# One PSUM ring of eight banks, bank-wise exp, larger loads and a new list of steps in a windowed-attention and gated-MLP kernel

## The chip, the cores and the metric

The kernel runs on one core of a Trainium2 chip. The metric is the device time of one execution in microseconds (us), lower is better. The engines are TensorE (PE in the profile, its weight loads PEld), VectorE (DVE), ScalarE (ACT), GpSimd (POOL) and SyncE (SP), which here only issues DMAs. Each engine works through its own instructions in order.

## What is computed

Eight batches of 576 positions go through causal attention with a window of 64 (8 heads of 64), and the result, laid out as 576 x 512, goes through a gated MLP with a spatial mixing matrix.

```python
scores = (1.0 / np.sqrt(D)) * np.matmul(q, k.transpose(0, 1, 3, 2))
mask = (rel >= 0) & (rel < 64)                     # rel = query position - key position
scores = np.where(mask, scores, -1000000000.0)
attn = softmax(scores)
x = np.matmul(attn, v)                             # (8, 8, 576, 64) -> (8, 576, 512)
h = np.maximum(x @ w_in, 0.0)                      # 512 -> 1024
u, vv = h[..., :512], h[..., 512:]
v_n = (vv - mean(vv)) / np.sqrt(var(vv) + 1e-06)   # over the last axis
v_s = np.einsum('ts,bsd->btd', w_spatial, v_n) + b_spatial[None, :, None]
out = (u * v_s) @ w_out                            # 512 -> 512
```

Inputs and output are float32; the kernel computes in float16 with float32 sums.

## The kernel before

The kernel is a set of named steps and one list, `ORDER`, which is written out by hand into the program: each word of it is a step, the engine that takes it, and the buffer numbers that it acquires (`S0_0:PE:0:1`). The steps are emitted in that order, so the list fixes the order of every engine's instructions; semaphores for the dependencies follow from the buffers.

The names of the steps, b the batch, g the group of four heads, u the pair of heads:

- `ldq`, `ldk` (L401), `ldv` (L422): loads of Q, K (one DMA of 576 KB for four heads) and V (five DMAs for four heads, one per 128 positions, in runs of 256 bytes). `ldwin`, `ldwsp`, `ldwo`, `ldb`: loads of the weights and the bias (L327, L343, L384, L352). All loads are issued by SP's queue, marked `DQ`.
- `cq`, `ck`: cast of Q, K to float16 (L293, L296, L301, depending on the engine); `tq`, `tk`: transpose on DVE (L408). `cv`: cast of V; `sl`, `su`, `s4`: copies of V shifted by 64 positions into `hs`.
- `S` (L470): scores of four heads, each head in a PSUM bank of its own. Two banks form a `pair` tile, and there are two pairs. `E` (L477): exp of one pair, 128 x 1024, on ACT. `M` (L480): mask by a minimum on DVE. `Z` (L493): sums over keys by a matmul with ones; `N`, `n` (L519, L521): log and exp of minus the log, that is, the reciprocal. `P` (L504): attention times V; `X` (L512): times the reciprocal. Steps with `_r` are the last 64 queries of a batch (L539, L549, L553, L562, L575, L583).
- `V` (L653, L666): the half of x @ w_in that is normalised, j = 0..3 for 128 positions each and j = 4 for the last 64; `Vr` (L633): relu on ACT; `Vb`, `Va` (L635, L637): mean and variance on DVE; `L1`, `L2` (L680, L682): one over the deviation; `A` (L692): normalisation on DVE. `U` (L708, L713): the other half, transposed; `Ur` (L721): relu. `W`, `We`: transpose of w_spatial on PE and its copies. `G` (L738, L744): spatial mixing; `Ge` (L752): times u. `O` (L763): output product; `Oe` (L610): copy to SBUF; `st`: store. `V_4` of a batch also computes the last 64 rows of the output of the batch before it (L669).
- `D` (L791): warm-up matmuls on a zero tile, which nothing reads.

PSUM holds eight banks: two pairs for the scores and four single banks for everything else. Loads of Q, K and of the weights share eight buffers `nat`; V has four buffers `natv` of four heads.

The list begins with Q and K of batch 0, then mixes V of batch 0 with Q and K of batch 1 and the weights:

```
ldq0_0:DQ:0 ldk0_0:DQ:1 D14:PE:0 ldk0_1:DQ:2 ldq0_1:DQ:3 D12:PE:1 ldv0_00:DQ:0 ldq1_0:DQ:4 D23:PE:2
ldk1_0:DQ:5 ldv0_10:DQ:1 D15:PE:3 cq0_0:POOL:0 ldv0_11:DQ D22:PE:0 D6:PE:1 tq0_0:DVE:0 D0:PE:2
```

Of the kernel before, what the change touches and what calls it, by code (L numbers as in the profile page):

```python
# [29 lines left out]
cv0_11:DVE ldwin001:DQ S1_0:PE:0:1 sl0_11:DVE X0_00:DVE:0 D20:PE:2 cwin110:POOL ldwin010:DQ:4  # L30
E1_00:ACT:1 s40_1:DVE D19:PE:0 ldwin011:DQ su0_11:POOL X0_01:DVE ldwsp3:DQ:5 E1_01:ACT:0 M1_00:DVE
cwin111:POOL P0_10:PE:1 P0_11:PE:2 X0_10:DVE:1 D18:PE:0 cwin100:ACT cwin101:POOL ldwsp2:DQ:7 D3:PE:3
n0_r:ACT X0_11:DVE cwin000:ACT Z1_00:PE:1 M1_01:DVE ldwsp1:DQ:6 P0_r:PE:0 cb:ACT V0_1:PE:3
X0_r:DVE:0 V0_2:PE:2 ck1_1:POOL:2 ldwsp4:DQ:0 Vr0_1:ACT:0 N1_00:ACT:5 Vb0_1:DVE:0 V0_0:PE:0
# [807 lines left out]
```

## Time and profile before

| | |
|---|---|
| median of 3 runs | 203.19 us (202.53 to 204.65) |
| span of the profiled execution | 201.0 us, first to last instruction; its device time is not listed apart, the median of the runs lies 2.2 us above the span |
| busy PE / PEld / DVE / ACT / POOL | 188.6 / 97.7 / 161.2 / 167.0 / 76.5 us |
| HBM read and written | 32.79 MB and 9.44 MB |

A row of the profile names the line, the engine, the operation, and out<-in with the shapes. A timeline row begins with its start and its length in us and merges instructions of one line that follow each other (x3 is three of them); what stands in brackets is the idle time before it and what ended it. Rows of stretches have no names in front; their columns are explained where they are shown.

### The profile page before, as it was taken

The page shows a single profiled execution, that of the slowest core. Times are in us where ns is not written, and L with a number is a line of the kernel's source. Part 1 is how long each engine was busy: PE and PEld are TensorE (multiplying, and loading weights), DVE is VectorE, ACT ScalarE, POOL GpSimd, SP SyncE. Part 2 cuts the span into 40 slices and gives each one's busy share as a digit, 9 for nine tenths or more (in the row PEclk, how much of TensorE's full clock was granted, in tenths as well). Part 3 has the DMA queues.
Part 4 walks back from the last instruction along what each step waited for, and adds up shares of the span by engine and source line. Part 5 has one row for each costly group of instructions (what it writes and reads, how often), then busy time and mean ns, then how long its engine had stood idle before and what let it go on. Part 6 is the DMA issues. An engine that isn't in the chain of part 4 may idle for free.

```text
span 201.0 us, 7008 instructions
## 1 busy us (share of the span) xinstructions
PE 188.6 (94%) x2927; PEld 97.7 (49%) x2927; DVE 161.2 (80%) x307; ACT 167.0 (83%) x307; POOL 76.5 (38%) x144
## 2 busy tenths in 40 slices
PE   7588889899999999989999999999999999999992
PEld 2233535545445445654455545554465455444450
DVE  4699979999998999699699898979957796647430
ACT  2588799878999899897998989999999999457431
POOL 5202575675894398153757999000000000000000
PEclk9999999999999999999999999999999999999998
DMA  6997999899898876999859995897633004200345
GB/s 221 387 276 184 336 378 210 292 372 377 185 274 255 246 221 188 295 243 234 311 118 262 241 316 178 227 284 249 185 111 117 3 5 132 108 0 0 128 145 202
DMA packets 50275, 42.69 MB, mean 212 GB/s; under 512 B 39361, under 2 KB 39489, under 8 KB 50242
## 3 DMA queue, kind: packets, MB, share of 16 engines
q1 hardware_dynamic: 50018, 41.91, 70.1%
q8 instruction: 23, 0.38, 0.8%
q10 hardware_dynamic: 224, 0.33, 0.5%
q14 instruction: 10, 0.08, 0.1%
HBM read 32.79 MB, written 9.44 MB: 210 GB/s over the span
## 4 chain that ended last, share of the span: by engine, by line
PE 70%; DMA 9%; SPq 7%; ACT 5%; DVE 5%; POOL 1%; issue 1%; POOLq 0%
PE bank L738 16%; PE bank L653 12%; PE bank L763 12%; PE bank L708 10%; DMA nk<-in_k_dram 9%; SPq L422 4%; PE pair L470 4%; PE bank L504 3%; PE bank L666 3%; PE bank L493 3%; PE bank L744 2%; SPq L327 2%; ACT e L477 1%; PE bank L713 1%; ACT ob L610 1%
## 5 line engine op out<-in xcount | busy, mean ns | idle before, releaser
L738 PE MATMUL bank<-wspT,vn 128*128 128x512 f16 (+1 forms) x160 | 37.5, 379 | 0.0
L477 ACT ACTIVATE e<-pair 128x1024 f16<-128x1024 f32 x32 | 31.9, 1027 | 2.7 <-PE pair L470 2.5
L752 DVE TENSOR_TENSOR g<-bank,ru 128x512 f16<-128x512 f32 (+1 forms) x40 | 24.8, 632 | 11.0 <-PE bank L738 5.0
L708 PE MATMUL bank<-x,win 128*128 128x512 f16 x128 | 31.6, 379 | 0.0
L763 PE MATMUL bank<-wout,g 128*128 128x512 f16 x128 | 31.3, 379 | 0.0
L653 PE MATMUL bank<-win,x 128*128 128x512 f16 x128 | 30.4, 379 | 0.2 <-DVE x L512 0.2
L721 ACT ACTIVATE ru<-bank 128x512 f32<-128x512 f32 (+1 forms) x40 | 21.4, 562 | 8.4 <-PE bank L708 4.6
L635 DVE BATCH_NORM_STATS2 st<-vs 128x6 f32<-128x512 f16 (+1 forms) x40 | 25.9, 670 | 3.0 <-ACT vs L633 2.8
L512 DVE TENSOR_TENSOR x<-bank,lz 128x512 f16<-128x512 f32 x32 | 21.2, 683 | 5.4 <-PE bank L504 2.6
L633 ACT ACTIVATE vs<-bank 128x512 f16<-128x512 f32 (+1 forms) x40 | 22.9, 597 | 3.1 <-PE bank L653 2.3
L610 ACT COPY ob<-bank 128x512 f32<-128x512 f32 (+1 forms) x39 | 22.6, 588 | 3.3 <-PE bank L763 3.1
L738 PEld LDWEIGHTS <-vn 128*128 128x128 f16 (+1 forms) x160 | 14.9, 97 | 17.7 <-DVE vn L692 0.5
L480 DVE TENSOR_TENSOR e<-e,mask 128x1024 f16<-128x1024 f16 x32 | 22.5, 721 | 1.0 <-ACT e L477 1.0
L408 DVE STREAM_TRANSPOSE qT<-hq 128x576 f32<-128x576 f32 x16 | 19.7, 1243 | 2.5 <-POOL hq L296 2.3
L296 POOL CAST hq<-nq 128x384 f16<-128x384 f32 x33 | 16.5, 536 | 13.1 <-DMA nq<-in_q_dram 12.5
L408 DVE STREAM_TRANSPOSE kT<-hk 128x576 f32<-128x576 f32 x16 | 20.0, 1247 | 1.4 <-ACT hk L293 1.1
L519 ACT ACTIVATE lz<-bank 128x512 f32<-128x512 f32 x32 | 18.6, 603 | 2.1 <-PE bank L493 2.0
L521 ACT ACTIVATE lz<-lz 128x512 f32<-128x512 f32 x32 | 19.6, 631 | 0.1
L653 PEld LDWEIGHTS <-x 128*128 128x128 f16 x128 | 12.0, 97 | 14.3 <-issue 0.6
L708 PEld LDWEIGHTS <-win 128*128 128x128 f16 x128 | 11.9, 98 | 14.4 <-issue 1.3
L763 PEld LDWEIGHTS <-g 128*128 128x128 f16 x128 | 11.8, 98 | 13.4 <-issue 0.5
L692 DVE TENSOR_SCALAR vn<-vs,mv,ln 128x512 f16<-128x512 f16 (+1 forms) x40 | 15.4, 436 | 3.5 <-ACT ln L682 3.3
(85 smaller groups left out, 294.7 us busy)
## 6 DMA issues: line engine op xcount, KB each, us to landing
nq<-in_q_dram SPq DMA_DIRECT2D x16, 576.0 KB, 6.4
nk<-in_k_dram SPq DMA_DIRECT2D x16, 576.0 KB, 5.5
nv<-in_v_dram SPq DMA_DIRECT2D x64, 128.0 KB, 4.9
out_dram<-ob SPq DMA_DIRECT2D x14, 512.0 KB, 4.6
wi<-in_moe_w_in_dram SPq DMA_DIRECT2D x8, 256.0 KB, 5.6
ws<-in_moe_w_spatial_dram SPq DMA_DIRECT2D x4, 288.0 KB, 8.2
nv<-in_v_dram SPq DMA_DIRECT2D x16, 64.0 KB, 3.6
wo<-in_moe_w_out_dram SPq DMA_DIRECT2D x4, 256.0 KB, 7.1
```

The source lines that it names most:

```text
L408: d = add(f"t{name}{b}_{g}", ("DVE", 1.09), key, lambda e: nc.vector.transpose(qt.t[:, :].rearrange("p (i j) -> p j i", j=18), h.t[:, :].b ...
L477: ex = add(f"E{b}_{g}{u}", ("ACT", 0.91), key, lambda e, u=u: nc.scalar.activation(e2[u].t[:, :, :], sc[u].t[:, :, :], AF.Exp, bias=0.0, s ...
L480: mins.append(add(f"M{b}_{g}{u}", ("DVE", 0.65), key, lambda e, u=u: nc.vector.tensor_tensor(e2[u].t[:, :, :], e2[u].t[:, :, :], mask[:, : ...
L610: lambda e: (nc.vector.tensor_copy if last else nc.scalar.copy)(view(), m.t[rows, 0:n]),
L633: rl = add(f"Vr{b}_{j}", ("ACT", 0.49), key, lambda e: nc.scalar.activation(vs.t[0:jn, :], m.t[0:jn, :], AF.Relu), deps=[pv], acq=[vs], us ...
L635: s1 = add(f"Vb{b}_{j}", ("DVE", 0.6), key + 0.02, lambda e: nc.vector.bn_stats(st6.t[0:jn, 0:6], vs.t[0:jn, :]), deps=[rl], acq=[st6], us ...
L653: nc.tensor.matmul(m.t[:, :], xr(b, r)[:, 128 * j:128 * j + 128], w_in_sb[r][:, 512:1024], start=(r == 0), stop=(r == 3))
L708: nc.tensor.matmul(m.t[:, :], w_in_sb[r][:, 128 * i:128 * i + 128], xr(b, r), start=(r == 0), stop=(r == 3))
L721: lambda e, m=m, ru=ru, n=n: nc.scalar.activation(ru.t[:, 0:n], m.t[:, 0:n], AF.Relu), deps=[pu], acq=[ru], uses=[m])))
L738: nc.tensor.matmul(m.t[:, :], w[0:kn, 128 * i:128 * i + 128], wspT[kk][0:kn, 0:512], start=(kk == 0), stop=(kk == 4))
L752: lambda e, m=m, g=g, ru=ru, n=n: nc.vector.tensor_tensor(g.t[:, 0:n], m.t[:, 0:n], ru.t[:, 0:n], ALU.mult),
L763: nc.tensor.matmul(m.t[:, :], G[r][0].t[:, 128 * j:128 * j + 128], w_out_sb[r][:, :], start=(r == 0), stop=(r == 3))
```

## The change

- PSUM becomes eight single banks, and every step takes any of them. A score step takes four banks, and exp works on one bank at a time: `E1_00` to `E1_03`, 128 x 512 each, and four of 128 x 128 for the last queries. The mask still works on two heads at once and waits for both exps.
- A weight load covers two blocks (512 KB, or 576 KB of w_spatial) where it was one. V is loaded for eight heads per DMA (two buffers `natv` of eight heads), for batch 0 in two groups of four heads as before. V's copies are one step per two blocks and eight heads; on POOL each is issued block by block.
- The first V steps of batch 0 are emitted in two halves, `V0a` (rows of w_in that meet heads 0 to 3) and `V0b`.
- 48 warm-up steps of one matmul take the place of 25 of two.
- The list is a new one. Q and K of batch 0 are followed by V of batch 0, the weights `win1`, `wsp`, Q of batch 1, `win0` and the rest of batch 1. In the steady part the order of all steps differs.

The heart of the diff:

```diff
 ORDER = """
-ldq0_0:DQ:0 ldk0_0:DQ:1 D14:PE:0 ldk0_1:DQ:2 ldq0_1:DQ:3 D12:PE:1 ldv0_00:DQ:0 ldq1_0:DQ:4 D23:PE:2
...
+ldk0_0:DQ:0 ldq0_0:DQ:1 ldk0_1:DQ:2 cq0_0:DVE:0 ck0_0:POOL:1 tk0_0:DVE:0 ldq0_1:DQ:3 tq0_0:DVE:1
+ldv0_00:DQ:0 D0:PE:0 D1:PE:1 D2:PE:2 D3:PE:3 D4:PE:4 D5:PE:5 D6:PE:6 D7:PE:7 D8:PE:0 D9:PE:0
...
+D21:PE:0 D22:PE:0 D23:PE:0 D24:PE:0 D25:PE:0 D26:PE:0 S0_0:PE:0:1:2:3 ck0_1:POOL:2 ldv0_01:DQ
+ldv0_10:DQ cq0_1:ACT:3 tk0_1:DVE:2 ldv0_11:DQ E0_00:ACT:0 ldv0_12:DQ cv0_00:ACT:0 E0_02:ACT:1
+ldv0_02:DQ ldv0_13:DQ tq0_1:DVE:3 ldv0_03:DQ cv0_10:DVE E0_03:ACT sl0_00:POOL:0 E0_01:ACT D27:PE:4
+D28:PE:4 D29:PE:4 D30:PE:4 D31:PE:4 D32:PE:4 S0_1:PE:4:5:6:7 M0_00:DVE D33:PE:0 D34:PE:0
+S0_r:PE:0:2:3:1 ldv0_04:DQ E0_12:ACT:2 ldv0_14:DQ E0_10:ACT:3 sl0_10:DVE E0_r0:ACT:0 ldwin10:DQ:4
+M0_01:DVE E0_11:ACT su0_00:POOL E0_13:ACT ldwin11:DQ:5 E0_r1:ACT ldwsp1:DQ:6 cv0_11:DVE D35:PE:6
+Z0_00:PE:6 D36:PE:4 Z0_01:PE:4 M0_10:DVE N0_00:ACT:0 M0_11:DVE cv0_01:DVE s40_0:DVE s40_1:DVE
+su0_11:DVE N0_01:ACT:1 su0_01:DVE E0_r2:ACT ldb:DQ:7 sl0_01:DVE n0_00:ACT D37:PE:0 D38:PE:0
+Z0_10:PE:0 D39:PE:5 Z0_11:PE:5 E0_r3:ACT su0_10:DVE ldwsp0:DQ:0 cwsp3:POOL N0_10:ACT:2 n0_01:ACT
+M0_r:DVE cwin100:ACT D40:PE:7 D41:PE:7 D42:PE:7 P0_00:PE:7 N0_11:ACT:3 sl0_11:DVE P0_01:PE:2
+P0_10:PE:6 Z0_r:PE:4 X0_00:DVE:0 P0_11:PE:3 n0_10:ACT cwin101:DVE N0_r:ACT:4 X0_01:DVE n0_11:ACT
+X0_10:DVE:1 ldwsp2:DQ:1 cwsp2:ACT cwin110:ACT ldq1_0:DQ:2 ldwin01:DQ:3 ldwin00:DQ:4 X0_11:DVE
+cwin111:DVE P0_r:PE:1 cwin001:POOL D43:PE:0 D44:PE:0 D45:PE:0 V0a_3:PE:0 cwsp0:DVE cwsp1:DVE
+ldk1_0:DQ:6 V0a_0:PE:7 n0_r:ACT V0a_1:PE:5 cb:ACT cwsp4:ACT D46:PE:2 V0b_1:PE V0b_0:PE V0b_3:PE
+V0a_2:PE:2 X0_r:DVE:0 Vr0_1:ACT:0 cq1_0:DVE:0 Vr0_3:ACT:1 cwin000:POOL Vr0_0:ACT:2 V0b_2:PE
...
-NWARM = 25
-BUFS = {"nat": 8, "natv": 4, "hqk": 4, "qkT": 6, "hv": 4, "hs": 4, "e2": 4, "er": 2, "lz": 6,
+NWARM = 48
+BUFS = {"nat": 8, "natv": 2, "hqk": 4, "qkT": 6, "hv": 2, "hs": 2, "e2": 4, "er": 2, "lz": 6,
...
-    PAIR = [psp.tile([128, 2, 512], f32, name=f"pair{i}") for i in range(2)]
-    SINGLE = [psp.tile([128, 512], f32, name=f"bank{i}") for i in range(4)]
+    BANKS = [psp.tile([128, 512], f32, name=f"bank{i}") for i in range(8)]
...
-        elif e == "POOL" and len(i.shape) == 4 and i.shape[1] > 2:
-            for lo, hi in ((0, 2), (2, i.shape[1])):
-                nc.gpsimd.tensor_copy(o[:, lo:hi, :, :], i[:, lo:hi, :, :])
+        elif e == "POOL" and len(i.shape) == 4 and i.shape[2] == 8:
+            for c in range(i.shape[1]):
+                nc.gpsimd.tensor_copy(o[:, c, :, :], i[:, c, :, :])
...
+                ld = add(f"ldwin{half}{g}", ("DQ", 0.4), kk,
+                         lambda e, st=st, g=g, cs=cs: nc.sync.dma_start(
+                             st.t[:, 0:1024].rearrange("p (f c) -> p f c", f=2),
+                             moe_w_in[256 * g:256 * g + 256, cs].rearrange("(f p) c -> p f c", f=2)),
+                         acq=[st], nbytes=1.6, n=256)
...
+        groups = [(0, 4), (4, 8)] if b == 0 else [(0, 8)]
...
+                         lambda e, c=c, sn=sn, h0=h0, h1=h1: nc.sync.dma_start(
+                             nv.t[0:sn, c, h0:h1, :],
+                             v[b, h0:h1, 128 * c:128 * c + sn, :].transpose([1, 0, 2])),
...
-            ex = add(f"E{b}_{g}{u}", ("ACT", 0.91), key, lambda e, u=u: nc.scalar.activation(
-                e2[u].t[:, :, :], sc[u].t[:, :, :], AF.Exp, bias=0.0, scale=0.125),
-                deps=[s], acq=[e2[u]], uses=[sc[u]])
+            ex = []
+            for w in (0, 1):
+                ex.append(add(f"E{b}_{g}{2 * u + w}", ("ACT", 0.48), key,
+                              lambda e, u=u, w=w: nc.scalar.activation(
+                                  e2[u].t[:, w, :], sc[2 * u + w].t[:, :], AF.Exp, bias=0.0,
+                                  scale=0.125),
+                              deps=[s] + ex, acq=[] if w else [e2[u]],
+                              uses=[sc[2 * u + w]] + ([e2[u]] if w else [])))
...
+            if b == 0:
+                halves = []
+                for f in (0, 1):
+                    def emit_H(e, j=j, m=m, f=f):
+                        with nc.named_scope(f"V{b}_{j}"):
+                            for r in (2 * f, 2 * f + 1):
+                                nc.tensor.matmul(m.t[:, :], xr(b, r)[:, 128 * j:128 * j + 128],
+                                                 w_in_sb[r][:, 512:1024], start=(r == 0), stop=(r == 3))
...
-            for _ in range(2):
-                nc.tensor.matmul(m.t[:, :], scratch[:, 0:128], scratch[:, :], start=True, stop=True)
-        add(f"D{i}", ("PE", 0.43), -2.0, emit_D, acq=[m], mode="f")
+            nc.tensor.matmul(m.t[:, :], scratch[:, 0:128], scratch[:, :], start=True, stop=True)
+        add(f"D{i}", ("PE", 0.22), -2.0, emit_D, acq=[m], mode="f")
```

Further on in the new list PE's order is: `V0_4`, the five `W`, `U0_4`, `U0_0` to `U0_3`, `S1_0`, `G0_1`, `G0_0`, `S1_1`, `G0_3`, `S1_r`, `Z1_00`, `Z1_01`, `G0_2`, `G0_4`, `Z1_11`, `Z1_r`, `Z1_10`, `O0_0`, `O0_3`, `O0_2`, `P1_r`, `P1_00`, `P1_10`, `P1_01`, `V1_4`, `P1_11`, `O0_1`, `S2_0`, `U1_4`, `V1_0`. DVE has, between the last `A0` and `V1_0`: `tq1_1`, `tk1_1`, the five masks of batch 1, the five `Ge0`, `cv1_0`, `su1_0`, `cv1_1`, `su1_1`, `tk2_0`, `tq2_0` and the five `X1`. Behind U0's casts POOL has `ck1_0`, `ck1_1`, three `cwo`, `ck2_0`, `sl1_1`, `cq2_0`, `cq2_1`, `ck2_1`. All of batch 0's `O` steps stand ahead of `V1_0`; in the old list they stand behind it.

More of the change, by code (lines that the diff above doesn't have):

```diff
@@ L30 @@
[L30 to L34, printed above, removed]
-Vr0_2:ACT:1 tk1_1:DVE:0 cq1_1:POOL:3 ldv1_00:DQ:2 V0_3:PE:3 Vr0_0:ACT:2 n1_00:ACT ldwsp0:DQ:2
@@ L455, in att_steps @@
     def att_steps(b, g, key):
[L456 removed]
+        sc = [buf("bank", f"sc{b}_{g}{hh}") for hh in range(4)]
         e2 = [buf("e2", f"e2_{b}_{g}{u}") for u in (0, 1)]
@@ L527, in rem_steps @@
     def rem_steps(b, key):
-        sc = [buf("pair", f"scr{b}_{u}") for u in (0, 1)]
+        sc = [buf("bank", f"scr{b}_{hh}") for hh in range(4)]
         def emit_S(e):
```

402 lines of the change are left out of this document (206 added, 196 removed).

## The prediction

> **What bounds the kernel now.** I read the page's head and engine shares first, then busy time by stretches, then the order of time on each engine in the first 50 us, then the DMA queue.
>
> ```profile
> span 201.0 us, 7008 instructions
> PE 188.6 (94%) x2927; PEld 97.7 (49%) x2927; DVE 161.2 (80%) x307; ACT 167.0 (83%) x307; POOL 76.5 (38%) x144
> ...
> 0.00:10.00 10.00, 6.68 (x83) 2.90 (x84) 5.80 (x17) 4.11 (x4) 3.74 (x14) 1.00 0.82 303
> 10.00:20.00 10.00, 8.42 (x164) 3.84 (x162) 9.87 (x19) 8.80 (x15) 1.14 (x2) 1.00 0.93 231
> 20.00:30.00 10.00, 8.62 (x136) 4.35 (x137) 8.64 (x14) 8.89 (x16) 6.40 (x12) 1.00 1.02 358
> 30.00:40.00 10.00, 9.16 (x196) 5.54 (x196) 9.94 (x26) 8.71 (x20) 6.01 (x10) 1.00 1.01 250
> ...
> 46.76:196.60 149.84, 148.66 (x2202) 76.97 (x2203) 120.31 (x225) 130.93 (x247) 54.78 (x99) 1.00 0.64 186
> ...
> 130.00:170.00 40.00, 39.91 (x591) 21.05 (x590) 31.27 (x62) 39.44 (x71) 0.00 (x0) 1.00 0.44 136
> ```
>
> The columns are the stretch, its length, the busy time of PE, PEld, DVE, ACT and POOL, then granted clock, DMA share and GB/s. From 46.76 on PE idles 1.2 us of 149.8, at full granted clock. In the last row ACT is 99% busy and PE still idles only 0.1: a nearly full ACT does not hold PE up if the list feeds it well. So the back is PE's own work, and the change does not take matmuls out of it. What can be won lies in the first 47 us, where DVE and the DMA queue are full and PE waits or runs warm-up matmuls.
>
> ```profile
> 8.67 0.76 PE L470 MATMUL pair<-qT,kT 32*64 32x128 f16 x64 [2.05 <-DVE kT L408]
> 24.62 3.63 PE L653 MATMUL bank<-win,x 128*128 128x512 f16 x16
> 39.91 0.76 PE L744 MATMUL bank<-wspT,vn 128*128 128x64 f16 x20 [0.40 <-DVE wspT L301]
> 46.76 2.75 PE L653 MATMUL bank<-win,x 128*128 128x512 f16 x12 [0.18 <-DVE x L512]
> 196.47 0.63 PE L776 MATMUL bank<-wout,g 128*64 128x256 f16 x8
> 147.13 0.47 PE bank L713 x16
> 193.09 3.47 PE bank L763 x16
> ```
>
> These are the milestones: first scores S0_0 at 8.67, V0 at 24.62, G0 at 39.91, V1 at 46.76, last matmul at 196.47. The last two rows (from the chain) price a U step of the 64-row rest at 0.47 and four O steps at 3.47, so 0.87 for one full step of four matmuls. When V1 starts at 46.76, none of the four O0 steps has run.
>
> **The change, part by part.** I lay the new list out by hand up to the first V1 step, with these rows.
>
> ```profile
> 4.84 1.40 POOL L296 CAST hq<-nq 128x384 f16<-128x384 f32 x3 [1.64 <-DMA nq<-in_q_dram]
> 6.13 1.15 ACT L293 CAST hk<-nk 128x1152 f16<-128x1152 f32 x1 [4.03 <-DMA nk<-in_k_dram]
> 10.10 0.75 DVE L301 CAST hq<-nq 128x1152 f16<-128x1152 f32 x1
> 72.89 2.32 DVE L408 STREAM_TRANSPOSE qT<-hq 128x576 f32<-128x576 f32 x2
> 9.48 1.94 ACT L477 ACTIVATE e<-pair 128x1024 f16<-128x1024 f32 x2 [0.52 <-PE pair L470]
> 157.14 1.55 ACT L633 ACTIVATE vs<-bank 128x512 f16<-128x512 f32 x3
> 16.19 1.59 ACT L519 ACTIVATE lz<-bank 128x512 f32<-128x512 f32 x3
> 15.65 0.66 ACT L549 ACTIVATE er<-pair 128x256 f16<-128x256 f32 x2 [0.70 <-PE pair L539]
> 11.99 1.26 DVE L480 TENSOR_TENSOR e<-e,mask 128x1024 f16<-128x1024 f16 x2
> 23.43 1.27 DVE L512 TENSOR_TENSOR x<-bank,lz 128x512 f16<-128x512 f32 x2
> 30.02 1.82 DVE L635 BATCH_NORM_STATS2 st<-vs 128x6 f32<-128x512 f16 x3
> 35.53 0.72 DVE L692 TENSOR_SCALAR vn<-vs,mv,ln 128x512 f16<-128x512 f16 x2
> 28.83 1.27 POOL L301 CAST win<-wi 128x512 f16<-128x512 f32 x2
> nq<-in_q_dram SPq DMA_DIRECT2D x1, 576.0 KB, 7.1
> 4.00:6.00 2.00, 2.00 (x9) 0.79 (x7) 0.00 (x0) 0.00 (x0) 1.16 (x3) 1.00 0.99 389
> 14.00:20.00 6.00, 5.35 (x90) 2.27 (x88) 5.91 (x14) 5.30 (x12) 1.14 (x2) 1.00 0.76 181
> ```
>
> *First scores.* The first load lands at 4.84, the second at 6.13, the fourth (issued at 2.20, 7.1 later) at 9.3; the four loads keep their place. K0 is now cast on POOL (4.84 to 6.25), Q0 on DVE (6.13 to 6.85), then two transposes at 1.1 and 1.2: S0_0 at 9.2, 0.5 later than before.
>
> *Exp bank by bank.* A run of n rows gives the spacing of one instruction: 0.91 for a 1024-wide exp (1.94 less 1.03), about 0.475 for a 512-wide one from PSUM to f16 (three in 1.55, the first 0.60), 0.50 to f32, 0.27 for 256. A split exp is 2 x 0.475 against 0.91: 0.04 more each, 32 of them 1.3 us of ACT. The 128-wide exp is not in the trace; between 0.15 (half of 256) and 0.27 I take 0.2, nearer the bottom because length still counts at 256, so 4 x 0.2 against 0.55, 2.0 over eight batches. If instructions did not overlap, a split would cost 2 x 0.60 less 0.91 = 0.29: that end is kept for a rival. ACT gets 3.3 us, 2.5 of it behind V1. These rows price what the list takes away from it behind V1:
>
> ```profile
> L293 ACT COPY hs<-hv 64x768 f16<-64x768 f16 (+3 forms) x12 | 9.6, 797 | 0.3 <-POOL hv L301 0.2
> L293 ACT CAST hs<-nv 64x256 f16<-64x256 f32 x10 | 4.0, 401 | 0.0
> ```
>
> Some 11 of these small V copies go to POOL or into fewer, wider ones (5 us), and four O0 evacuations and two wout casts move ahead (3): about 8.
>
> The Trainium skill, "ScalarE: Activation LUTs", section "Rules for kernel authors", budgets about 0.3 us per ACTIVATE plus 0.83 ns per element, so every split would cost 0.3: an estimate by that page of 14 us for the 48 added instructions. The rows disagree as long as instructions follow each other closely; the last but one rival is what would hold if they did not.
>
> *ACT until V0.* From 9.3 ACT has, in list order up to the last weight copy: one cast 1.1, eight exps 3.8, four small ones 0.8, one V cast 0.5, five logs and five exps of the sums 4.6, five weight and bias copies 2.75; 13.5 in all, so 22.8, and 20.3 at the last wide reciprocal. Then X0_11 and a weight cast on DVE (0.6 + 0.4, DVE itself ends 22.0). V0a runs before that on half the heads, so V0 is four half steps and V0_4 from 22.0: it ends at about 25.1. Before, it started only at 24.62. Splitting V0 costs nothing: it is the same matmuls. The new waits at the head of ACT are V0's first pair of loads (due about 10.6, that is 8.0 for Q and K, 2 x 0.65 and 1.3 until the semaphore; needed at 10.8, seven exps behind it) and win10 (needed at 18.0).
>
> *DMA.* Bytes and packets stay the same (V still goes in 256-byte runs), so fewer, larger loads save only issues. What moves is the order: 1.2 MB of batch 1 goes behind the weights. Q and K of batch 0 (2.36 MB) at 389 GB/s end at about 8, V0 (1.18 MB) at 181 to 200 GB/s at about 14.2, and I add 1.2 for issues that SP can only write when V has drained. Then win1, wsp, q1_0, win0: 4.0 MB in 10.3, plus 1.3 until the semaphore: win00 at 27.0 (25.8 without the 1.2). POOL casts it (2 x 0.64) until 28.3: U0 from 28.3 to 32.3, S1_0 to 33.0. K1_0 lands 1.5 behind win00, is cast on POOL until 29.9 and transposed until 31.0; five normalisations at 0.36 follow: G0 at 33.0. Warm-up matmuls fill only these waits (one delays a ready step by 0.2 at most).
>
> *G0 to V1.* From here DVE sets the pace: four transposes at 1.08, four masks at 0.6 (1.26 less 0.65) and one at 0.35, as much for X and for gating (spacing 0.6, nearly the X row's), two V casts at 0.7 and two shifted copies at 0.65: 15.3, so V1 at 48.3. The 1024-wide copies are bounded by 0.5 and 0.8 (twice a 512-wide one). PE's work in that stretch, G0, S1_1, S1_r, sums, P1, the O0 steps, V1_4, S2_0, U1_4, is 13.5: it fits under DVE.
>
> *The sum.* V1 starts 1.5 later than before (48.3 against 46.8), but four O0 steps (3.47), V1_4 (0.87) and U1_4 (0.47) are done: 4.8 of PE work. The rest, 149.8 - 4.8 = 145.0, follows at the pace of before: PE ends at 193.3 instead of 196.6. The ring of eight banks and the new list have nothing to win behind that, since only 1.2 us of idle time is left there. Tail unchanged: span 197.7. The median of 203.19 lies 2.2 above the span shown, so **199.9 us**, 3.3 less. Bounds: 1.2 less if SP keeps ahead; 0.3 either way for the copies.
>
> **The rivals.**
>
> ```profile
> 4.63 8.55 SPq L422 DMA_DIRECT2D nv<-in_v_dram  x6
> 14.71 2.05 SPq L422 DMA_DIRECT2D nv<-in_v_dram  x3
> 57.39 2.69 DVE L692 TENSOR_SCALAR vn<-vs,mv,ln 64x512 f16<-64x512 f16 x5
> 57.48 1.39 POOL L299 CAST hv<-nv 128x512 f16<-128x512 f32 x2
> 51.52 0.96 DVE L480 TENSOR_TENSOR e<-e,mask 128x1024 f16<-128x1024 f16 x1
> ```
>
> *Slower: V0 blocks SP's queue.* All ten V0 loads now stand ahead of the weights. Six of them took 8.55, 1.43 each. At that pace they end at 2.7 + 14.3 = 17.0, win10 lands about 5 later at 22, and ACT, which reaches its cast at 18.0 with the sums of batch 0 queued behind, stalls 4. The weights and V1's loads (as many V bytes again, for cv1 at the head of DVE) are late by the same rate: 2.5 more. 199.9 + 6.5 = 206.4. It decides against the change from 3.3 on. For it: the row. Against it: in that stretch 1.2 MB of Q and K (3 us) went through first, and the three later ones took 0.68 each.
>
> *About the same: DVE stretched by POOL.* Beside POOL's V casts five normalisations took 2.69, 0.52 each instead of 0.36, and a mask 0.96 instead of 0.65. In the DVE-bound 33 to 48 POOL now casts Q2, K2 and wout: five masks at +0.3 and the copies give 2 late: 201.9.
>
> *About the same: exps that do not overlap.* 24 wide and 12 pairs of small exps after V1 at up to 0.29 and 0.2 more are 9.4 us. ACT then asks 130.9 - 8 + 9.4 = 132 of 145, but nearly all before 170, where it is full: 2 on PE, 201.9. Against it: the runs above.
>
> *Nothing comes of it:* the lead is eaten in PE's order by a bank wait or the last loads: 203.2. For it: behind V1 ACT is busy 87% of the time (130.93 of 149.84) and DVE 80%, so there is not much room to be late in. Against it: the row of 130 to 170.
>
> **How the numbers follow.** Forecast, with its own range 198.0 to 201.2 (the bounds and half a microsecond of idle time either way): 0.58. SP's queue: 0.17. POOL beside DVE: 0.10. Exps: 0.05. Nothing: 0.06. Faster still, below 197.5, because the new banks also remove the small stalls and SP keeps ahead: 0.04. A measurement here tells about 1%, 2 us: below 201.2 is faster (0.62), above 205.2 slower (0.17), between them 0.21. The range goes from 197.0 to 205.4; it leaves out most of the SP case and some of the last.
>
> **What would show it.** Right: S0_0 near 9.2; the first V0 matmul near 21, V0_4 done by 26; G0 near 33; V1 near 48 with O0 before it; PE idle under 2 us from there; 512-wide exps spaced 0.48 in runs. Wrong: ACT or SP idle for DMA of win or nv between 12 and 30 (SP's case); exps spaced above 0.55; normalisations near 0.5 at 31 to 33; PE idle over 4 us behind V1, with a bank's evacuation as releaser.

## The result: slower by 2.9%

The changed kernel takes 208.96 us (median of four runs, 208.39 to 209.29) where the kernel before takes 203.1 beside it: a ratio of 1.0291 with a 95% interval of 1.0241 to 1.0341. Forecast were 199.9 us and a range of 197.0 to 205.4. The profiled execution has a span of 206.9 us, 9.2 more than the 197.7 of the sum.

The first view is the page's head, then busy time by stretches, with the columns of the prediction's first fence (stretch, length, PE, PEld, DVE, ACT, POOL, granted clock, DMA share, GB/s).

```profile
span 206.9 us, 6969 instructions
PE 190.8 (92%) x2925; PEld 98.5 (48%) x2925; DVE 163.2 (79%) x310; ACT 163.2 (79%) x342; POOL 82.9 (40%) x144
...
0.00:10.00 10.00, 8.26 (x92) 3.76 (x93) 6.02 (x18) 1.78 (x2) 5.17 (x17) 1.00 0.85 282
10.00:20.00 10.00, 8.86 (x199) 4.38 (x198) 9.14 (x21) 10.00 (x24) 1.09 (x2) 1.00 0.89 238
20.00:30.00 10.00, 7.80 (x49) 3.62 (x46) 6.71 (x13) 7.11 (x15) 1.53 (x3) 1.00 1.04 361
...
53.20:202.90 149.70, 145.34 (x2171) 75.35 (x2170) 117.89 (x218) 124.13 (x263) 59.43 (x94) 0.99 0.60 173
50.00:60.00 10.00, 7.93 (x158) 4.09 (x144) 6.99 (x10) 6.41 (x15) 8.39 (x15) 0.83 1.05 268
...
90.00:100.00 10.00, 7.85 (x204) 4.56 (x209) 9.33 (x13) 7.27 (x14) 7.97 (x13) 1.00 1.08 328
130.00:170.00 40.00, 39.73 (x614) 21.31 (x601) 30.76 (x60) 36.84 (x77) 2.39 (x4) 1.00 0.32 101
```

Behind V1 ACT does 6.8 us less than before (124.13 against the 130.93 of the prediction's first fence; 8 less and 2.5 more were forecast), and from 130 on PE is as full as before. The hole is between: PE does 7.9 us of work in 50 to 60, at a granted clock of 0.83, and 7.9 in 90 to 100. One row for the whole stretch of both kernels shows its size, the kernel before first:

```profile
26.00:103.00 77.00, 74.84 (x1328) 39.91 (x1327) 70.25 (x128) 69.76 (x135) 50.00 (x91) 1.00 0.92 266
```

```profile
26.00:103.00 77.00, 69.78 (x1262) 36.93 (x1261) 71.49 (x121) 66.77 (x144) 54.93 (x93) 0.98 1.00 290
```

PE did 5.1 us less in these 77 us, which is nearly the size of the difference of the spans (5.9). DVE was busier and got through seven instructions fewer.

PE's order of time (start, length, idle time before it) and then PE's list of waits show where it stood:

```profile
25.66 1.05 PE L708 MATMUL bank<-win,x 128*64 128x512 f16 x4 [1.19 <-DVE x L611]
30.36 0.64 PE L755 MATMUL bank<-x,win 128*128 128x64 f16 x16 [0.99 <-POOL win L301]
35.08 2.12 PE L780 MATMUL bank<-wspT,vn 128*128 128x512 f16 x9
49.35 0.82 PE L493 MATMUL bank<-qT,kT 32*64 32x128 f16 x58
52.18 0.31 PE L493 MATMUL bank<-qT,kT 32*64 32x128 f16 x6 [2.00 <-issue]
53.27 3.80 PE L681 MATMUL bank<-win,x 128*128 128x512 f16 x12
94.28 0.76 PE L493 MATMUL bank<-qT,kT 32*64 32x128 f16 x63
97.07 0.21 PE L493 MATMUL bank<-qT,kT 32*64 32x64 f16 x1 [2.04 <-issue]
...
PE bank L493 <- issue: 4.0, 2, 2.0
PE bank L708 <- DVE x L611: 1.2, 1, 1.2
```

V0_4 starts at 25.66, U0_4 at 30.36, G0 at 35.08, V1 at 53.27. Twice PE stops for 2.0 us in the middle of a score step, after 58 of S2_0's 64 matmuls and before the last of S4_1, and the releaser is "issue": nothing that the profile shows. Behind the first stop twelve V matmuls take 3.80 us that took 2.75 before. The kernel before has one wait for issue, of 0.5 us.

### The profile page after: what moved, and what is told of

It is laid out like the page before. It is cut to its first block, busy times and chain, and to the rows that moved or that the text cites. A ratio compares the mean times of both kernels' runs of the same rounds, so it can differ in the third digit from the quotient of the medians.

```text
span 206.9 us, 6969 instructions
## 1 busy us (share of the span) xinstructions
PE 190.8 (92%) x2925; PEld 98.5 (48%) x2925; DVE 163.2 (79%) x310; ACT 163.2 (79%) x342; POOL 82.9 (40%) x144
## 4 chain that ended last, share of the span: by engine, by line
PE 43%; DVE 29%; ACT 12%; DMA 8%; issue 4%; SPq 1%; ACTq 0%
PE bank L780 11%; PE bank L681 9%; DMA nq<-in_q_dram 8%; PE bank L805 6%; DVE vn L734 5%; PE bank L750 5%; DVE st L663 4%; DVE x L540 4%; DVE e L508 4%; DVE qT L413 3%; DVE kT L413 3%; ACT e L503 3%; PE bank L493 3%; ACT vs L661 2%; DVE g L794 2%
## 5 line engine op out<-in xcount | busy, mean ns | idle before, releaser
L503 ACT ACTIVATE e<-bank 128x512 f16<-128x512 f32 x64 | 35.4, 611 | 5.9 <-PE bank L493 5.0
L780 PE MATMUL bank<-wspT,vn 128*128 128x512 f16 (+1 forms) x160 | 38.8, 380 | 1.1 <-DVE vn L734 0.6
L663 DVE BATCH_NORM_STATS2 st<-vs 128x6 f32<-128x512 f16 (+1 forms) x40 | 26.7, 679 | 7.8 <-ACT vs L661 7.3
L299 POOL COPY hs<-hv 64x512 f16<-64x512 f16 x35 | 24.8, 735 | 17.9 <-PE bank L603 12.8
L681 PE MATMUL bank<-win,x 128*128 128x512 f16 x112 | 27.9, 390 | 0.0
L508 DVE TENSOR_TENSOR e<-e,mask 128x1024 f16<-128x1024 f16 x32 | 24.4, 784 | 3.3 <-ACT e L503 3.3
L296 POOL CAST hk<-nk 128x384 f16<-128x384 f32 x39 | 21.2, 579 | 12.5 <-DMA nk<-in_k_dram 4.8
L549 ACT ACTIVATE lz<-lz 128x512 f32<-128x512 f32 x32 | 20.4, 666 | 0.1
L734 DVE TENSOR_SCALAR vn<-vs,mv,ln 128x512 f16<-128x512 f16 (+1 forms) x40 | 16.7, 471 | 4.1 <-ACT ln L724 4.0
L493 PE MATMUL bank<-qT,kT 32*64 32x128 f16 (+2 forms) x1024 | 13.3, 226 | 6.0 <-issue 4.0
```

The source lines that it names most:

```text
L503: lambda e, u=u, w=w: nc.scalar.activation(e2[u].t[:, w, :], sc[2 * u + w].t[:, :], AF.Exp, bias=0.0, scale=0.125),
L508: mins.append(add(f"M{b}_{g}{u}", ("DVE", 0.65), key, lambda e, u=u: nc.vector.tensor_tensor(e2[u].t[:, :, :], e2[u].t[:, :, :], mask[:, : ...
L663: s1 = add(f"Vb{b}_{j}", ("DVE", 0.6), key + 0.02, lambda e: nc.vector.bn_stats(st6.t[0:jn, 0:6], vs.t[0:jn, :]), deps=[rl], acq=[st6], us ...
L681: nc.tensor.matmul(m.t[:, :], xr(b, r)[:, 128 * j:128 * j + 128], w_in_sb[r][:, 512:1024], start=(r == 0), stop=(r == 3))
L734: ENG[e].tensor_scalar(o[0:jn, :], VS[j].t[0:jn, :], mv_t[b % NSB][0:jn, j, 0:1], ln.t[0:jn, 5 + j:6 + j], ALU.subtract, ALU.mult)
L780: nc.tensor.matmul(m.t[:, :], w[0:kn, 128 * i:128 * i + 128], wspT[kk][0:kn, 0:512], start=(kk == 0), stop=(kk == 4))
```

## The experiments

**What the two stops have in common.** Both rows below are busy time from the start to a stop:

```profile
0.00:50.15 50.15, 44.12 (x735) 22.24 (x735) 41.89 (x87) 37.61 (x78) 20.90 (x46) 1.00 0.97 301
0.00:95.00 95.00, 85.37 (x1503) 44.12 (x1503) 82.24 (x155) 76.29 (x161) 56.36 (x104) 0.98 0.96 285
```

The stops stand behind matmul 735 and matmul 1503, and 1503 less 735 is 768, six times 128. The list of DMA queues has one that moves instructions (packets, MB, share):

```profile
q8 instruction: 23, 0.38, 0.8%
```

23 packets of 16 KB for 2925 matmuls are one for 127 matmuls with their weight loads. The queues between 46.3 us, where PE passes the last border of 128 matmuls ahead of the first stop, and 49.5:

```profile
q1 hardware_dynamic: 1630, 1.09, 112.5%
issues: line engine op xcount, KB each, median us to landing
```

and from 49.5 to 52:

```profile
q1 hardware_dynamic: 857, 0.70, 108.0%
q8 instruction: 1, 0.02, 3.3%
```

For 3.2 us after that border no instruction packet moves; the loads fill the queues. The packet begins at 49.54, and PE goes on at 52.18. The second stop is alike: PE passes the border before it (matmul 1375) at 90.65, the packet begins at 94.86, and PE goes on at 97.07. My theory was that PE had run out of instructions; the rival, that something in S2_0 and S4_1 stops it.

**1. The border moved by 64 matmuls, twice.** Warm-up matmuls were cut into narrower ones.

```
-nc.tensor.matmul(m.t[:, :], scratch[:, 0:128], scratch[:, :], ...)
+nn = 4 if i < 16 else 2 if i < 32 else 1
+for c in range(nn): ...   # columns 512 // nn * c and on
```

> The changed kernel, with 32 of its warm-up matmuls written as two or four narrower ones: 64 more matmuls (128 more PE instructions) in the first 9 us, the same elements through PE, everything behind them unchanged. Theory A (PE waits for its own instructions: the packets of kind instruction, 16 KB each, that the profile lists in a queue of their own): the place where PE runs out moves 64 matmuls earlier in the program, so the 2.0 us at 52.2 us behind the 58th matmul of S2_0 and the 2.0 us at 97.1 us in S4_1 are gone from these places; what is left of them stands 64 matmuls earlier or has vanished; 204 to 208.5 us. Rival B (something in S2_0 and S4_1, their banks or their operands, stops PE): both stalls at the same matmuls, 2.0 us each, 208.5 to 209.5 us.

> The same kernel as the first shift (64 matmuls more), timed in five rounds to put an interval on it. If the 205.96 us of its four runs is real: 204 to 206.5 us, a ratio of 1.005 to 1.02 against the kernel before, below the changed kernel's 1.029; if those runs were luck: 207 to 209 us.

The first time 205.96 us (203.69 to 208.63, before 202.72), the second 205.78 (204.73 to 207.24, before 202.99), a ratio of 1.0148, 1.0091 to 1.0206, which does not touch the changed kernel's interval. Nothing stops at the old places. In the second, two shorter waits for issue are left, 1.1 us at 13 us and 0.8 at 69; PE's list of waits, and its busy time up to the later of the two:

```profile
PE bank L493 <- issue: 2.0, 2, 1.1
PE bank L521 <- DVE e L508: 1.5, 1, 1.5
...
PE bank L780 <- DVE vn L734: 1.1, 2, 0.9
...
0.00:69.25 69.25, 62.87 (x1119) 37.30 (x1119) 59.68 (x119) 55.34 (x116) 35.55 (x71) 1.00 1.00 298
```

1119 is 735 and three times 128, counted with the 64 new matmuls. The stop goes with the count of instructions, not with a step. That is theory A, and 3 us. The same count over the twenty profiles of this case says the same: of 44 idle times of PE over 0.1 us whose releaser is "issue", 42 stand behind a number of matmuls that leaves 95 when divided by 128, as 735 and 1503 do; the other two, in the kernel before and in its variant of experiment 6, leave 94.

**2. Fewer bytes of V.** `h0:h1` became `h0:1` in the V loads of batches 2 to 7.

> The changed kernel, whose V loads of batches 2 to 7 fetch 1 head of 8 (the other seven keep the values of an earlier batch in the same slot): some 7 MB less through the DMA queues, all engines' work the same. Theory A (the instruction packets wait behind the loads in full DMA queues): both stalls of 2.0 us gone, and with the first the low granted clock of the slice 50 to 60 us: 203.0 to 205.5 us. Rival B (the packets are late whatever the queues carry, because short matmuls use up 16 KB faster than a packet comes): both stalls stay, 208 to 209.5 us. Under both the first 35 us stay as they are, since batch 0 and 1 are loaded whole.

208.23 us (206.87 to 209.62), 1.0299 (1.0215 to 1.0382): no change, where theory A had 203.0 to 205.5. Both stops are there, 1.7 us each, again behind matmuls 735 and 1503. The run did not tell the theories apart, because the queues stayed full where it mattered: the q and k loads moved up, and DMA share was 1.02 in 40 to 50 and 1.03 in 90 to 100.

**3. Fewer bytes of everything.** So q and k were cut as well.

```
-n.t[:, :], src[...]
+n.t[:, 0:1152 if b < 2 else 256], src[...][:, 0:1152 if b < 2 else 256]
```

> The changed kernel with loads of batches 2 to 7 cut: 256 of 1152 columns of q and k, 1 head of 8 of V (the rest keeps older values), and eight small memsets on POOL ahead of its first cast. DMA share in 45 to 110 us falls from about 1 to some 0.3. Theory A1 (the packet waits behind loads in full queues): packets begin within 1 us of a block's start, both stalls gone or under 1 us, 203.5 to 206 us. Theory A2 (a block of 3.7 us is eaten faster than any packet comes, full queues or not): both stalls stay at 1.5 us or more, 207 to 209.5 us.

> The changed kernel with the loads of batches 2 to 7 cut as before (256 of 1152 columns of q and k, 1 head of 8 of V), with two small memsets on DVE in place of the eight on POOL, so that S0_0 starts at 9.2 us as in the changed kernel. In the first light kernel S0_0 came 3.0 us late and PE ended 0.4 us earlier than in the changed kernel. If emptier queues are worth what was seen behind S0_0: no stall without a releaser over 1 us behind 40 us, 204.5 to 207 us. If the time comes back as other waits: 207.5 us and more.

In the first, the memsets held up the first loads and S0_0 came 3.0 us late: 210.32 us (208.68 to 213.85), by estimate 207.3 without those 3.0, and no wait for issue is left in its profile. The second took 206.16 (204.92 to 208.25), 1.0144 (1.0071 to 1.0216). No wait for issue is left in its list of PE's waits either. The queues in the 2.1 us behind the same border (45.9 to 48.0):

```profile
q1 hardware_dynamic: 547, 0.32, 54.9%
q8 instruction: 1, 0.02, 3.7%
```

The packet begins 0.5 us behind the border in place of 3.3. With the same instructions at the same places, emptier queues take both stops away: full queues make the packets late.

**4. The border moved by 96 and by 120.** The same cut with other numbers.

> The changed kernel with 32 warm-up matmuls written as four narrower ones each: 96 matmuls (192 PE instructions) more in the first 10 us, nothing else. In the profile of the changed kernel PE runs out behind matmul 735 and behind matmul 1503, 768 apart, which is 12 blocks of 16 KB less 6, that is 6 blocks of 128 matmuls; and the packets of kind instruction begin 0.1 to 4.3 us after a block of 128 matmuls is entered. Theory A (PE runs out where it finishes a block of 128 matmuls before the next but one packet has come): counted from the trace, the shortest block ahead of 110 us is then 4.7 us long instead of 3.7 and 4.2, so no stall of 2 us is left, at most 1 us in all: 203.5 to 206 us. Rival B (stalls belong to steps or to the time of day): two of 2.0 us, 208 to 209.5 us.

> The changed kernel with 24 warm-up matmuls written as five and 8 as four: 120 matmuls more, so that the borders of the blocks of 128 matmuls fall 8 matmuls later in the program than in the changed kernel: behind the whole of S2_0 instead of behind its 58th matmul. Counted from the trace, the shortest block ahead of 110 us is then 4.9 us (at 86 us, where DMA share is 0.54) and none in 40 to 80 us is under 5.9. Theory A (PE ends a block before the packet that it needs has come): no stall without a releaser over 1 us behind 15 us; the stretch from S2_0's first matmul to the 800th (7.9 us in the changed kernel) takes 4.5 us; 203.5 to 206.5 us. Rival (what the stall took comes back as waits for DVE and ACT): stall gone, 207 to 209 us.

209.13 us (1.0322, 1.0235 to 1.0409) and 208.51 (1.0294, 1.0237 to 1.0351): no gain, against the theory's 203.5 to 206.5. The stops of 2 us are gone, but PE's waits (of the 120) show what stands in their place:

```profile
PE bank L689 <- ACT win L293: 2.6, 1, 2.6
PE bank L521 <- DVE e L508: 2.0, 2, 1.4
...
PE bank L755 <- issue: 1.1, 1, 1.1
PE bank L681 <- issue: 0.7, 1, 0.7
...
PE bank L567 <- issue: 0.7, 1, 0.7
```

Shorter stops at other borders (behind matmuls 863, 991 and 1631, which are 735 and 1, 2 and 7 times 128), and a new wait of 2.6 us in the front, for a weight cast that stands behind late DMA. Fetching 96 or 120 matmuls earlier did not cause that by any step that I can show; the kernel with half the mask work (experiment 10), which adds no matmul, has the same wait:

```profile
PE bank L689 <- ACT win L293: 2.3, 1, 2.3
```

From S2_0's first matmul (number 677) to the last one the changed kernel takes 153.6 us, the one with 96 more 151.1 and the one with 120 more 152.0. So the back did gain 2.4 and 1.6; but they reach S2_0 2.6 and 1.4 us later (51.92 and 50.77 against 49.35), and that takes the gain away. My count of block lengths foresaw where the long stops vanish, not what the whole takes.

**5. The same shift in the kernel before.**

> The kernel before with 24 of its 50 warm-up matmuls written as five narrower ones: 96 matmuls more, nothing else. Counted from its trace, the shortest block of 128 matmuls is then one of 2.7 us that begins at 61 us (it was 4.2 us at 82 us). Theory A (a block that PE finishes faster than its packet comes): a stall of 1 to 3 us with nothing as releaser at about 64 us, which the kernel before does not have: 203.5 to 206 us. Rival B (the changed kernel's steps or banks): no such stall, 202.5 to 203.5 us.

203.83 us, 1.0047 (0.9997 to 1.0098). At 64.2 us, where the kernel before has nothing, PE now waits for issue, but 0.55 us and not 1 to 3 (two others, 0.9 us at 15.8 and 0.5 at 88.1, stand at such borders, too):

```profile
64.23 0.22 PE L504 MATMUL bank<-e,hv 128*64 128x64 f16 x2 [0.55 <-issue]
```

The packet began 1.0 us behind its border at 60.8. So a short block alone is cheap here; the long stops had a packet that was 3 us late, too. The place is theory A's, the size was a miss.

**6. Split exponentials in the old order.**

```
-nc.scalar.activation(e2[u].t[:, :, :], sc[u].t[:, :, :], AF.Exp, ...)
+[nc.scalar.activation(e2[u].t[:, w, :], sc[u].t[:, w, :], AF.Exp, ...) for w in (0, 1)]
```

> The kernel before, in its own order and with its pairs of banks, but each exponential of two banks written as two of one bank (48 more ACT instructions). By the spacing of 0.49 us that the changed kernel's profile shows for 512 wide ones, against 0.94 of one of 1024: +0.04 us each, 2 us of ACT in all and ACT is not the bound at most of these places: 202.5 to 204.5 us. Rival (an instruction costs some 0.3 us of its own and ACT sets the end of its stages): 206 us and more.

202.79 us, 1.0025 (0.9985 to 1.0066): nothing to measure. In the order of ACT's work, four in a row and in the changed kernel five:

```profile
9.42 2.06 ACT L477 ACTIVATE e<-pair 128x512 f16<-128x512 f32 x4 [0.69 <-PE pair L470]
```

```profile
11.56 2.55 ACT L503 ACTIVATE e<-bank 128x512 f16<-128x512 f32 x5
```

**7. The front's order.** `ldwin01 ldwin00` ahead of `ldq1_0` on SP; `Vr0_1 Vr0_3 Vr0_0` ahead of `cwsp4` on ACT; `X0_r Vb0_3` ahead of `cwsp0 cwsp1`, and `Vb0_1 Vb0_0` ahead of `cq1_0`, on DVE.

> The changed kernel with the second half of w_in fetched ahead of q of batch 1, ACT's relus of V0 ahead of its cast of the last wsp rows, and on DVE the normalisation of the 64 last rows and three statistics ahead of work that waits for a landing. Theory A (the 2.9 us that the front lost against the forecast are landings of weights and what queued behind them): U0_4 at 28 to 29 us instead of 30.36, G0 at 33 to 34 instead of 35.08, and 206.5 to 208 us in all, as long as the stalls at 52 and 97 us stay. Rival B (the front is bound by DVE's run from 26.4 to 35.5 us whatever lands): G0 at 35, 208.5 to 209.5 us.

U0_4 comes at 28.03 and G0 at 34.0, as theory A has it:

```profile
24.18 1.05 PE L708 MATMUL bank<-win,x 128*64 128x512 f16 x4
...
28.03 0.63 PE L755 MATMUL bank<-x,win 128*128 128x64 f16 x16
...
34.00 0.82 PE L780 MATMUL bank<-wspT,vn 128*128 128x512 f16 x3 [0.43 <-DVE vn L734]
```

The whole took 207.38 us (207.15 to 209.47), 1.0279 (1.0203 to 1.0356): of 2.3 us at U0_4, 1.1 are left at G0, where DVE is late next, and 1.5 at the end of that profile; the interval does not tell it from the changed kernel.

**8. Half of batch 0's V from ACT's queue,** to get SP through: `(nc.scalar if h0 else nc.sync).dma_start`, with these five loads ahead of ACT's first cast.

> The changed kernel, with the five V loads of heads 4 to 7 of batch 0 issued from ACT's queue ahead of ACT's first cast instead of from SP's; nothing else. In the profile of the changed kernel SP spends 10.70 us on ten V loads (1.07 each) and issues the first half of w_in at 13.40 us. Theory A (the front waits for SP to get through these loads): w_in is issued at about 8 us, its first cast on ACT comes before 16 us instead of at 18.05, V0_4 at 23 to 24 us instead of 25.66, U0_4 at 27 to 28.5 instead of 30.36; 206 to 207.5 us. Rival B (the queues carry no more in that time, so weights land when they did): U0_4 at 30 us and 208 to 209.5 us.

> The same five loads from ACT's queue, and the order of the front changed as in the run before it (second half of w_in ahead of q of batch 1, relus and normalisation ahead of what waits for a landing). With U0_4 at 27 us and G0 at 32 to 33 us the whole is 2 to 3 us below the changed kernel, with one or two PE stalls of up to 2 us still in it: 204.5 to 207 us. If the front is bound by DVE's run instead: as the front's order alone, 207 to 208 us.

> Both changes of the front, and 20 warm-up matmuls written as five narrower ones: 80 matmuls more, which by the trace of the front's order leaves no block of 128 matmuls shorter than 4.7 us behind 8 us. Theory: no stall of 2 us without a releaser, some of about 1 us left where DMA is full, and the time behind V1 about 3 us shorter than in the changed kernel: 201 to 204.5 us. Rival (what the stalls took is taken again by ACT and DVE): within 1 us of the same kernel without the 80 matmuls.

210.45 (1.0342, 1.0275 to 1.041), 210.3 and 208.94 us (1.0205, 1.0111 to 1.0298): no gain on the changed kernel that the intervals show, and none of the three inside what was expected of theory A. SP's next loads did go out sooner, but q of the second half of batch 0 was then behind V, and S0_1 waited:

```profile
14.90 0.77 PE L493 MATMUL bank<-qT,kT 32*64 32x128 f16 x64 [2.39 <-DVE qT L413]
```

That is 2.9 us later than the 12.0 of the changed kernel, and U0_4 at 30.78 is no earlier. Rival B had that place right, though not the time (208 to 209.5); since S0_1 came late as well, the run does not show by itself that only the queues' rate holds the weights back.

**9. Both losses together.**

> The order of the front changed (second half of w_in ahead of q of batch 1, relus and normalisation ahead of what waits for a landing) and the 120 matmuls more. Alone, the order of the front ended 1.5 us earlier than the changed kernel in its profile. Independent losses: 202 to 205 us. Losses that take each other's place: 206 to 208.5 us.

209.18 us, 1.0302 (1.0248 to 1.0357). They do not add; a score step of batch 0 met a stop of 1.0 us for issue at 13.5 us, and between U0 and G0 PE waited 1.4 us for DVE's transpose of k.

> The order of the front changed as before (second half of w_in ahead of q of batch 1, relus and normalisation ahead of what waits for a landing) and 96 more matmuls in the warm-up together. If the two losses are independent: no stall of 2 us and the front 1.5 us shorter: 201.5 to 204 us, beside 202.7 of the kernel before. If the front's gain is lost again behind: 203.5 to 206 us.

208.8 us (206.72 to 211.91), much as its sister. Both times lie above all that was expected.

**10. Who takes the time back?** In busy time of the 77 us, the second kernel with 64 matmuls more:

```profile
26.00:103.00 77.00, 71.96 (x1277) 37.58 (x1276) 72.72 (x125) 69.76 (x151) 55.47 (x96) 1.00 1.02 295
```

DVE is busy 94% of it. The minimum with the mask takes 856 ns in the changed kernel and 712 before (groups of DVE's instructions in 26 to 107; busy, mean):

```profile
L480 DVE TENSOR_TENSOR e<-e,mask 128x1024 f16<-128x1024 f16 x15 | 10.4, 712 | 0.3 <-ACT e L477 0.3
```

```profile
L508 DVE TENSOR_TENSOR e<-e,mask 128x1024 f16<-128x1024 f16 x16 | 13.3, 856 | 1.7 <-ACT e L503 1.7
```

So POOL got less to do (`for n in (0, 384, 768)` became `(0,)` for batches 2 to 7), and in another kernel DVE (the mask on `e2[u].t[:, 0, :]` alone).

> The changed kernel, whose POOL casts of q and k of batches 2 to 7 convert one third of the columns (the rest keeps older values): some 12 us of POOL work less between 45 and 115 us, DVE, ACT and PE as they were. In the changed kernel's profile the minimum with the mask on DVE (16 in 26 to 107 us) takes 856 ns against 712 before, and DVE is busy nearly without a break from 26 to 103 us. Theory C (DVE sets the pace of that stretch and POOL's casts stretch its minima): mean down to 700 to 760 ns, DVE 1.5 to 2.5 us shorter up to 103 us, 206 to 207.8 us with the two PE stalls still there. Rival D (PE sets the pace): minima shorter, time 208.5 to 209.5 us.

> The same one third of POOL's casts of q and k, with the 64 matmuls more that move the blocks' borders (alone: 205.8 us). Theory C: the two losses are one chain, PE's stall costs what it makes DVE wait and POOL what it makes DVE longer, so the gains add: 203 to 204.8 us. Rival: the shift has already taken all there is: 205.3 to 206.5 us.

> The changed kernel, whose minimum with the mask works on one of the two banks only (the other stays unmasked): 32 instructions of 128x512 in place of 128x1024, some 0.4 us each, so that 6 us of DVE work are gone up to 103 us; PE, ACT and POOL as they were. Theory C (DVE sets the pace from 26 to 103 us): 3 to 5 us less, 204 to 206 us, with the PE stalls still there. Rival D (PE, its stalls and ACT set the pace): less than 1 us, 208 to 209.5 us.

Less POOL work: 208.52 us, 1.0307 (1.0202 to 1.0412). The minima fell to 794 ns, not to 700 to 760, and DVE's busy time in 26 to 103 from 71.49 to 70.27 us with two instructions more; but PE stopped for issue 4.2 us in that profile, and the time did not move. With the 64 matmuls more: 204.48 (203.73 to 207.31), 1.011 (1.0005 to 1.0214), 1.3 below the 64 matmuls alone (0.8 by the ratios), by intervals that overlap. Half the mask work: 209.51 us, with runs from 205.62 to 213.21; its profiled run was the 205.62. That scatter leaves theories C and D both open; its profile is looked at once more in the second table below.

The table puts PE's progress of several profiles side by side: the time in us at which the matmul starts that has n others ahead of it in the changed kernel's program (added warm-up matmuls not counted).

| n (step) | changed | 64 more | again | 120 more | emptier queues | front |
|---|---|---|---|---|---|---|
| 677 (S2_0) | 49.35 | 49.00 | 49.98 | 50.77 | 49.30 | 48.39 |
| 800 (S2_1) | 57.28 | 53.34 | 54.25 | 56.24 | 53.56 | 54.76 |
| 1119 | 75.91 | 73.99 | 74.56 | 74.98 | 75.92 | 73.03 |
| 1600 | 106.91 | 103.35 | 104.67 | 106.53 | 106.40 | 104.94 |
| 2924 (last) | 202.91 | 199.26 | 200.60 | 202.73 | 202.36 | 201.40 |

From 677 to 800 the first stop and the slow matmuls behind it cost 3.6 us (7.93 against 4.34, 4.27 and 4.26). From 1600 on all take 96 us (95.9 to 96.5). Between them, 800 to 1600 takes 49.6 in the changed kernel with its second stop of 2.04 us, and 50.0, 50.4 and 52.8 in the three that have no stop there: the second stop costs nothing that shows. What takes its place is the wait of the sums of batch 4 for DVE's mask, 1.5 us, in the list of waits under 1. In the profile with emptier queues all 3.7 us are lost again by the 1119th; there the minima take 986 ns, and the granted clock fell to 0.77 in 60 to 65 us. That execution took 208.25 us where the median of its kernel is 206.16, so its ending is not leant on.

A second table cuts the same profiles at the prediction's milestones (us; "idle" is PE's idle time behind V1). The forecast of the third row is the 150.1 of the kernel before, measured the same way, less the 4.8 of work done ahead.

| | forecast | changed | 64 more | again | emptier queues | half the mask |
|---|---|---|---|---|---|---|
| G0 starts | 33.0 | 35.1 | 34.6 | 35.7 | 35.4 | 36.7 |
| G0 to V1 | 15.3 | 18.2 | 15.8 | 15.6 | 15.2 | 15.7 |
| V1 to the last matmul | 145.3 | 149.6 | 148.9 | 149.3 | 151.8 | 147.5 |
| idle in the row above | 1.2 | 4.4 | 4.8 | 4.9 | 5.3 | 3.5 |

Without the long first stop, G0 to V1 takes what was forecast. Behind V1 no kernel comes near the forecast: where the stops for issue are shorter or gone, waits that end with DVE take their place (3.5 of the 4.9 us in "again", 1.4 of the 4.4 in the changed kernel, 0.6 of the 1.2 in the kernel before). With half the mask work 0.3 us of waits for DVE are left, and 2.9 us for issue. That fits theory C for the back, but it rests on one profile of a kernel whose times scatter.

## Why the prediction was wrong, by its own steps

*First scores*: 9.17 against 9.2. *Exp bank by bank*: spacing (2.55 less 0.59) / 4 = 0.49 against 0.475; with the run in the old order (202.79 us, 1.0025), the forecast near nothing holds, and the 14 us by the Trainium skill's page "ScalarE: Activation LUTs" (section "Rules for kernel authors") do not.

*ACT until V0 and DMA*: V0 began at 20.10 (forecast near 21), win10 reached ACT's cast at 18.05 as forecast, so the rival "V0 blocks SP's queue" failed in its place: ACT did not stall there. Its 206.4 us lie nearer to the result than the forecast does, but 4 of its 6.5 us are that stall, so the nearness is chance; its other 2.5, weights late by V's rate, came as 2.1 at win00:

```profile
2.66 10.70 SPq L435 DMA_DIRECT2D nv<-in_v_dram  x10
...
24.45 0.83 DVE L301 CAST wnat<-ws 128x576 f16<-128x576 f32 x2 [2.49 <-DMA ws<-in_moe_w_spatial_dram]
25.19 0.42 DVE L611 TENSOR_TENSOR x<-bank,lz_r 128x256 f16<-128x256 f32 x1
29.13 1.18 POOL L301 CAST win<-wi 128x512 f16<-128x512 f32 x2 [7.45 <-DMA wi<-in_moe_w_in_dram]
```

Ten V loads at 1.07, between my two ends, and all later landings 2 us behind: win00 at 29.1 against 27.0. I had put "V0_4 from 22.0" without what stands ahead of X0_r on DVE, two casts that waited 2.49 for wsp; it started at 25.66, where I had it ending at 25.1. G0 came 2.1 late. That term is mis-sized. Loads that landed late are shown; whether the queues' rate or SP's time per load makes them late isn't, since the three kernels that relieved SP made S0_1 late in its place.

*G0 to V1*: 15.3 of DVE was forecast and 18.2 came (35.08 to 53.27), of which 2.0 are the first stop; the kernels without it took 15.2 to 15.8, so the term itself was right. The sentence "PE's work in that stretch ... fits under DVE" is right in sum and silent on the stop.

*The sum*: the 9.2 us by which the span missed are 2.1 up to G0, 2.9 from G0 to V1 and 4.4 behind V1, less 0.2 in the tail. The step that failed is the last and largest of these, "the rest, 145.0, follows at the pace of before": V1 to the last matmul took 150.1 before and 149.6 now, so the 4.8 us of work done ahead brought nothing. PE's work is as forecast: 148.66 less the 4.8 done early is 143.9, and 145.34 came, 1.05 of it the slow V1 matmuls; but PE stands idle 4.4 of 149.70 us instead of 1.2 of 149.84. I had taken the near-gapless PE of the old list for a property of the back, while it was one of that list's mix: in 26 to 103 the new list has DVE at 93% and PE at 91% where it was 91% and 97%. "PE idle over 4 us behind V1" stood among the signs of being wrong, but with a bank's evacuation as releaser. It came with another: 2.0 of these 4.4 us are the second stop, and waits that end with a copy out of a bank are 0.4 us or less each. No run took the ring of eight banks away by itself, so what it costs or wins is not shown.

The rival "DVE stretched by POOL" is seen (856 against 712 ns, sixteen times 0.14, 2.3 us) and taking 62 of the 144 ns away did not move the time by itself. None of my rivals had PE waiting for its own instructions, and the sum put that term at nothing. The Trainium skill, "Runtime: NRT & Kernel Launch", section "Instruction fetch mechanics", says that an engine's instructions are refilled in blocks of 16 KiB, 256 instructions, through a DMA queue of the sequencer's own, and that the cost of crossing such a border is mostly hidden. The first part agrees with the trace (23 packets, one for 127 pairs of load and matmul); the second doesn't here, with 2.0 us in sight twice.

*What is shown and what stays open.* Of the 5.9 us of median that the change lost, 2.8 to 3.2 go when the first stop goes, whether its border is moved by 64 (205.96, 205.78) or the queues are emptied (206.16). The other 3 remain in all of these. In the two kernels with 64 more, V1 starts 3.6 and 4.5 us later than in the kernel before (50.4 and 51.3 against 46.8), with 4.8 us of work done ahead, and behind V1 they take 149 us where the kernel before takes 150: 4.8 and 4.9 us of idle time there, against 1.2 before, take up what the work done ahead should have won. Part of V1's lateness is the front, where G0 came 1.6 and 2.7 us later than forecast. No run took away the front's loss or the waits for DVE and kept the gain, and shifts by 96 and 120, which removed the long stops too, lost at the front what they gained behind it. Why the front loses up to 2.6 us to weights in some of these stays open, and so does what DVE's pace alone is worth. No kernel here was faster than the one before; the best whole one is the changed kernel with 64 matmuls more.

## What to carry to other kernels

A wait whose releaser is "issue" in the middle of a run of short matmuls: count the matmuls up to each such stop; if, with one weight load to each matmul, the counts differ by multiples of 128, PE waits for its instructions, and the place moves when instructions are added or taken away ahead of it. Here it cost most where many short matmuls stood in one block while loads filled the queues. That the new list pays more for it because it packs score steps together and sends larger loads is my reading; no run took the larger loads back. And a stretch in which PE has no gaps shows that the old list is balanced there, not that any other order of the same work will be: sum every engine's work stretch by stretch for the new order before the back is carried over as a constant.

## What the runs showed of the hardware that I had not expected

- From the start of a late instruction packet to PE's next matmul it took 2.2 to 2.7 us in each stop that I followed (94.86 to 97.07, 49.54 to 52.18), of which the packet itself took 1.0 to 1.3.
- The granted clock fell to 0.83 in the 10 us of the first stop: to 0.50 from 51.99 to 55.40, that is for 3.41 us, which is why the twelve V matmuls were slow. The second stop, as long, left it at 1.00. In steps of 3.41 us counted from that drop, the first stop lies almost whole in one step, and the second is spread over two (changed kernel, columns as in the first view):

```profile
48.57:51.98 3.41, 1.53 (x62) 0.88 (x59) 3.41 (x6) 2.00 (x4) 3.41 (x8) 1.00 1.17 280
52.00:55.38 3.38, 3.20 (x27) 1.71 (x28) 2.15 (x4) 2.06 (x4) 2.03 (x4) 0.50 1.13 224
...
92.95:96.35 3.40, 2.08 (x79) 1.19 (x75) 3.17 (x6) 2.54 (x6) 2.69 (x6) 1.00 1.07 348
96.37:99.75 3.38, 2.68 (x13) 1.19 (x13) 2.94 (x4) 2.17 (x4) 3.12 (x4) 1.00 1.12 330
```

PE idles 1.88 us in the first of these steps and 1.3 and 0.7 in the last two. In the twenty profiles every step at full clock with 1.88 us or more of idle time, seven in all, is followed by one at 0.50, and of those with less only one is (1.61 us; the longest that is not has 1.86). So by these profiles the idle time within one step counts, and not the length of a stop alone.
- A 128x1024 minimum in f16 on DVE took 712 to 986 ns in the mean of sixteen, by kernel; less POOL work brought 856 to 794.
- Two queues for V did not shorten the front: S0_1, which needs a load of q that was then behind V, came 2.9 us later.
